# Half-batch units in a fused chunk-select attention and gated FFN kernel: one fp32 transpose of keys and queries, chunk bounds taken from PSUM

## The chip, the cores and the metric

The kernel runs on one core of a Trainium2 chip. Times are device microseconds (us). Verdicts use a 95% interval of the ratio to the kernel before, measured on the same chip in the same rounds; "faster" needs more than 2%. A ratio is the mean time of one kernel's runs over that of the other's in the same rounds, so it is not quite the ratio of the medians that are quoted beside it.

Engine names in the profile: PE is the matmul engine, PEld its weight loads, DVE the vector engine, ACT the scalar engine, POOL GpSimd, SPq the queue that issues ordinary loads. The granted clock (PEclk) is the share of its full speed that PE was allowed. PSUM is the memory in which the matmuls and transposes of this kernel leave their results; its buffers come in small pools, and a slot is one buffer of a pool. "Early" and "late" unit below mean the first and the second half of a batch's queries. Units are named 0a, 0b, 1a and so on.

## The reference

Four batches, eight heads, 768 positions of 64 numbers. Keys are grouped into 24 chunks of 32. For each query, a bound on the score of each chunk is computed from the chunk's elementwise minimum and maximum; the six chunks with the highest bound, of those that causality allows, are kept, and softmax attention runs on them alone. The result goes through a gated FFN (512 to 1536 to 512).

```python
ub = np.sum(np.maximum(q[..., None, :] * k_min, q[..., None, :] * k_max), axis=-1)
ub = np.where(causal, ub, -1e9)
top_chunks = np.argsort(ub, axis=-1)[..., -6:]
scores = np.where(sel & lower_triangle, scale * (q @ k.T), -1e9)     # cut
attn = softmax(scores) @ v
gate = 1 / (1 + np.exp(-(x @ w_gate)))                               # x: heads side by side
out = (gate * (x @ w_val)) @ w_out
```

## The kernel before

A group is one batch and four of its heads. Keys are loaded twice, once by rows and once by chunks; the second copy feeds two long DVE reductions. Queries are transposed in fp32 for the bounds and, with the keys, a second time in fp16 for the scores. The mask of rejected chunks rides inside the score matmul as 32 more rows of the contraction (rows 64 to 96 of `hk` and `hq`). The FFN of batch b is mixed into the attention of batch b+1, so, apart from a few matmuls that run ahead, it begins when both groups of batch 0 are done.

```python
def load(g):                                       # one group: q, k, v by rows, k again by chunks
    nc.sync.dma_start(d["kc"], k[b, h0:h0 + 4].rearrange("h (c s) d -> (h c) s d", s=CH))
    for n, src in (("q", q), ("k", k), ("v", v)):
        for h in range(4):
            nc.sync.dma_start(d[n][:, :, h, :], src[b, h0 + h].rearrange("(sb p) d -> p sb d", p=128))

def chunk_bounds(g):                               # two DVE instructions over [96, 64, 32]
    nc.vector.tensor_reduce(kmm[:, 0:64], kv, AX.X, ALU.max)
    nc.vector.tensor_reduce(kmm[:, 64:128], kv, AX.X, ALU.min, negate=True)

# ... q_signs: fp32 transposes of q, relu(q) and relu(-q); feats: fp16 transposes of k and q (cut)

for g in range(NG):
    if g % 2 == 0 and g > 0:
        ffn = ffn_tasks(g // 2 - 1)                # the FFN of the whole batch before
        parts = [ffn[:len(ffn) // 2], ffn[len(ffn) // 2:]]
    a = attend_tasks(g, prep_tasks(g + 1))         # scores and values, preparation of the next group
    merge(a, parts[g % 2])                         # PE order: attention and FFN, mixed
for c, t in ffn_tasks(B - 1):
    t()                                            # the last FFN has nothing to mix with
```

The softmax here doesn't subtract the row's maximum and nothing guards it: scores larger than these inputs give would overflow.

## Time and profile before

| | before |
|---|---|
| median time | 393.64 us (393.15 to 393.91, 3 runs) |
| PE busy over the span | 320.2 us, 81% |
| first FFN product complete (its first matmul ran at 68.5) | 110.5 us |
| one group in the steady part | 41.35 us, PE busy 37.3 |
| FFN with nothing beside it, at the end | about 47 us |

These are lines of the page of the kernel before: busy time by engine, then PE, the granted PE clock in tenths, and the DMA engines, each in 40 equal slices of the span (a digit 9 is 90% or more).

```profile
span 393.6 us, 6906 instructions
PE 320.2 (81%) x2696; PEld 197.2 (50%) x2696; DVE 230.0 (58%) x486; ACT 204.6 (52%) x393; POOL 73.5 (19%) x77
...
PE   1071549287598999799979998799999999999996
PEclk9996557856969999999999999999999999999999
DMA  9999999297920964433615010002000100100102
```

The first eleven slices (108 us) are the start. There PE is partly idle, the DMA engines are full for seven slices, and the clock is low in much of it. From the twelfth slice PE reads 7 to 9 up to the last.

The windows view gives the same by stretches. Its columns are the length of the stretch, then busy time (and instruction count) of PE, PEld, DVE, ACT and POOL, the granted clock, the DMA share and GB/s. The first stretch is the start, the second one group of the steady part, the third the FFN at the end.

```profile
core 0: us, PE busy (x) PEld busy (x) DVE busy (x) ACT busy (x) POOL busy (x), PEclk, DMA share, GB/s
0.00:112.00 112.00, 57.58 (x502) 38.40 (x503) 76.61 (x156) 48.12 (x86) 35.86 (x43) 0.77 1.03 187
178.90:220.25 41.35, 37.30 (x338) 22.93 (x337) 27.81 (x60) 25.23 (x50) 8.08 (x7) 1.00 0.41 97
344.00:391.00 47.00, 45.98 (x260) 25.13 (x257) 13.29 (x24) 15.34 (x30) 0.00 (x0) 1.00 0.09 34
```

In the start PE is busy half the time; a steady group has 37.3 of 41.35 us; the end 46.0 of 47.

The groups view shows the two reductions of one steady group: busy us, mean ns of one.

```profile
L140 DVE TENSOR_REDUCE kmm_2829<-kc_2777 96x64 f32<-96x2048 f32 x1 | 3.7, 3680 | 0.0
L141 DVE TENSOR_REDUCE kmm_2829<-kc_2777 96x64 f32<-96x2048 f32 x1 | 3.6, 3583 | 0.0
```

### The profile page before, as it was taken

Reading aid. Unit: us, or ns where it says so; the run is one execution under the profiler, and the core shown is the slowest. Engines: PE = TensorE matmul, PEld = TensorE weight load, DVE = VectorE, ACT = ScalarE, POOL = GpSimd, SP = SyncE. Lnnn points to the kernel's source line nnn. Section 1 sums busy time; section 2 is a strip of 40 time slices with the busy share of each in tenths; the row PEclk is TensorE's granted clock in tenths of the full one; section 3 lists DMA queues with packets and bytes.
Section 4 is the critical chain, followed back from the end, with each engine's and each line's share of the span. In section 5 each row is a group of like instructions: output and inputs, shape, how many; then the busy total and the mean of one; then the engine's idle time right before and its main releaser. Section 6 shows DMA issues by size and latency. Waiting matters only on the chain.

```text
span 393.6 us, 6906 instructions
## 1 busy us (share of the span) xinstructions
PE 320.2 (81%) x2696; PEld 197.2 (50%) x2696; DVE 230.0 (58%) x486; ACT 204.6 (52%) x393; POOL 73.5 (19%) x77
## 2 busy tenths in 40 slices
PE   1071549287598999799979998799999999999996
PEld 0040335164464656455645555465666566565552
DVE  4947629967949745855596658664556544142230
ACT  1150446266576548555556656655876466332331
POOL 4504143232312051003300230011101001000000
PEclk9996557856969999999999999999999999999999
DMA  9999999297920964433615010002000100100102
GB/s 181 217 214 214 208 212 195 66 217 148 214 62 15 226 156 108 101 62 86 155 42 120 28 55 0 2 2 80 2 2 27 55 2 1 55 27 28 54 2 80
DMA packets 84400, 36.62 MB, mean 93 GB/s; under 512 B 75920, under 2 KB 80528, under 8 KB 83600
## 3 DMA queue, kind: packets, MB, share of 16 engines
q1 hardware_dynamic: 79616, 31.47, 37.3%
q0 software_dynamic: 4752, 4.72, 7.2%
q8 instruction: 21, 0.34, 0.4%
q14 instruction: 11, 0.09, 0.1%
HBM read 34.60 MB, written 6.29 MB: 104 GB/s over the span
## 4 chain that ended last, share of the span: by engine, by line
PE 58%; DVE 17%; ACT 8%; issue 6%; SPq 5%; DMA 4%; POOL 1%; ACTq 0%; DVEq 0%; POOLq 0%
SPq L125 5%; DMA k_177<-in_k_dram 3%; DMA kc_151<-in_k_dram 2%; DVE kmm_1096 L140 1%; DVE kmm_209 L140 1%; DVE kmm_721 L141 1%; DVE kmm_1096 L141 1%; DVE kmm_209 L141 1%; PE o_0_0_2626 L296 1%; PE o_0_0_3781 L296 1%; PE o_384_0_3203 L296 1%; PE o_384_0_2048 L296 1%; PE o_0_0_1471 L296 1%; PE o_384_2_4783 L296 1%; PE o_384_1_4298 L296 1%
## 5 line engine op out<-in xcount | busy, mean ns | idle before, releaser
L287 PEld LDWEIGHTS <-wv_146 128*128 128x128 f16 x384 | 37.9, 99 | 28.3 <-issue 4.2
L281 PEld LDWEIGHTS <-wg_145 128*128 128x128 f16 x384 | 35.7, 99 | 23.2 <-issue 6.7
L153 PE MATMUL qT_0_212<-ident_103,q_148 128*128 128x128 f32 x5 | 1.3, 426 | 8.4 <-DMA q_148<-in_q_dram 8.4
L243 PEld LDWEIGHTS <-hk_123 96*128 96x128 f16 x48 | 4.8, 122 | 3.8 <-issue 2.9
L153 PE MATMUL qT_1_227<-ident_103,q_148 128*128 128x128 f32 x5 | 1.3, 427 | 5.9 <-DVE qcat_1_221 L160 5.9
L153 PE MATMUL qT_0_369<-ident_103,q_176 128*128 128x128 f32 x5 | 1.3, 426 | 5.8 <-DMA q_176<-in_q_dram 5.8
L140 DVE TENSOR_REDUCE kmm_1096<-kc_1044 96x64 f32<-96x2048 f32 x1 | 3.7, 3667 | 3.7 <-PE kct_756 L146 3.7
L272 PE MATMUL xps_1_671<-ident_108,xnat_400 128*128 128x128 f16 x6 | 0.8, 307 | 6.1 <-DVE xnat_400 L265 6.1
L140 DVE TENSOR_REDUCE kmm_209<-kc_151 96x64 f32<-96x2048 f32 x1 | 3.6, 3591 | 3.8 <-DMA kc_151<-in_k_dram 3.8
L272 PEld LDWEIGHTS <-xnat_400 128*128 128x128 f16 x24 | 2.1, 120 | 7.2 <-DVE xnat_400 L265 6.9
L243 PEld LDWEIGHTS <-hk_135 96*128 96x128 f16 x48 | 4.3, 109 | 2.4 <-issue 1.1
L290 DVE SCALAR_TENSOR_TENSOR hg_384_0_4595<-gate_384_0_4588,v_384_0_4590 128x384 f16<-128x384 f16 x1 | 0.6, 553 | 8.5 <-PE v_384_0_4590 L287 8.5
L243 PEld LDWEIGHTS <-hk_125 96*128 96x128 f16 x48 | 4.5, 110 | 1.9 <-issue 0.5
L193 PEld LDWEIGHTS <-ap_140 128*128 128x128 f16 x20 | 1.5, 106 | 7.7 <-DVE ap_140 L187 6.1
L264 DVE RECIPROCAL rz_0_423<-pv_0_401 128x6 f32<-128x6 f32 x1 | 0.2, 195 | 8.8 <-PE pv_0_401 L261 8.8
L193 PE MATMUL apT_316<-ident_108,ap_140 128*128 128x128 f16 x5 | 0.7, 309 | 5.7 <-DVE ap_140 L187 5.7
L243 PEld LDWEIGHTS <-hk_131 96*128 96x128 f16 x48 | 4.1, 107 | 2.3 <-issue 1.1
L243 PEld LDWEIGHTS <-hk_133 96*128 96x128 f16 x48 | 4.3, 108 | 1.8 <-issue 0.2
L153 PEld LDWEIGHTS qT_0_212<-ident_103,q_148 128*128 128x128 f32 x5 | 0.9, 220 | 8.3 <-issue 8.3
L140 DVE TENSOR_REDUCE kmm_359<-kc_179 96x64 f32<-96x2048 f32 x1 | 3.6, 3597 | 2.4 <-DMA kc_179<-in_k_dram 2.4
L261 PE MATMUL pv_0_401<-v_141,att_0_335 128*128 128x65 f16 x21 | 1.3, 244 | 4.5 <-POOL att_0_335 L249 4.5
L243 PEld LDWEIGHTS <-hk_127 96*128 96x128 f16 x48 | 4.2, 106 | 1.6 <-issue 0.2
(2400 smaller groups left out, 1201.9 us busy)
## 6 DMA issues: line engine op xcount, KB each, us to landing
wg_145<-in_moe_w_gate_dram POOLq DMA_DIRECT2D x3, 512.0 KB, 9.8
wv_146<-in_moe_w_val_dram POOLq DMA_DIRECT2D x3, 512.0 KB, 7.7
wo_147<-in_moe_w_out_dram POOLq DMA_DIRECT2D x3, 512.0 KB, 12.9
kc_151<-in_k_dram SPq DMA_DIRECT2D x1, 768.0 KB, 5.9
q_148<-in_q_dram SPq DMA_DIRECT2D x4, 192.0 KB, 6.6
k_149<-in_k_dram SPq DMA_DIRECT2D x4, 192.0 KB, 6.5
v_150<-in_v_dram SPq DMA_DIRECT2D x4, 192.0 KB, 7.3
kc_179<-in_k_dram SPq DMA_DIRECT2D x1, 768.0 KB, 17.0
```

Source lines behind the costliest of these rows:

```text
L125: nc.sync.dma_start(d[n][:, :, h, :], src[b, h0 + h].rearrange("(sb p) d -> p sb d", p=128))
L140: nc.vector.tensor_reduce(kmm[:, 0:64], kv, AX.X, ALU.max)
L141: nc.vector.tensor_reduce(kmm[:, 64:128], kv, AX.X, ALU.min, negate=True)
L153: nc.tensor.transpose(ps[:, 128 * i:128 * i + 128], d["q"][:, i + 1, 2 * pr:2 * pr + 2, :].rearrange("p h d -> p (h d)"), ident32)
L193: nc.tensor.transpose(ps[:, 128 * i:128 * i + 128], apt[g % 2][:, i, :, :].rearrange("p h c -> p (h c)"), ident16)
L243: nc.tensor.matmul(ps[:, o:o + w], hk[:, 128 * jb:128 * jb + 128], hq[:, i0:i0 + w], start=True, stop=True)
L261: nc.tensor.matmul(ps[:, ib, :], at[:, c:c + 128], v16s[g % 2][:, jb, h, :], start=(jb == 0), stop=(jb == ib))
L272: nc.tensor.transpose(ps[:, 128 * ib:128 * ib + 128], xnat[b][:, ib, 128 * c:128 * c + 128], ident16)
L281: nc.tensor.matmul(gp, wg16[:, c, 128 * fb:128 * fb + 128], xT[(b, c)][:, t0:t0 + TCH], start=(c == 0), stop=(c == 3))
L287: nc.tensor.matmul(vp, wv16[:, c, 128 * fb:128 * fb + 128], xT[(b, c)][:, t0:t0 + TCH], start=(c == 0), stop=(c == 3))
L290: nc.vector.scalar_tensor_tensor(hg, gate, 1.0, vp, ALU.add, ALU.mult)
L296: nc.tensor.matmul(op, hgl[(b, t0, fc)][:, 128 * tb:128 * tb + 128], wo16[:, fc, :], start=(fc == 0), stop=(fc == NFB - 1))
```

## The change

The unit becomes half a batch of queries for all eight heads. Keys and queries are transposed once, in fp32. The chunk maximum and minimum are reduced straight from the PSUM of the key transpose, so the second key load and the fp16 casts of keys and queries on POOL go. The FFN of a unit is mixed into the attention of the next unit. The score matmul keeps its mask rows.

```diff
-def load(g):   # kc by chunks, then q, k, v of four heads
+def load(u):   # k, q, v of 384 rows, all heads
+    for n, src in (("k", k), ("q", q), ("v", v)):
+        for i in range(HB):
+            nc.sync.dma_start(t[:, i], src[u.b, :, r:r + 128].rearrange("h p d -> p h d"))
-    nc.vector.tensor_reduce(kmm[:, 0:64], kv, AX.X, ALU.max)
-    nc.vector.tensor_reduce(kmm[:, 64:128], kv, AX.X, ALU.min, negate=True)
+def keys_t(u, p, pool):             # a pair of heads
+    ps = pool.tile([128, T], F32, tag="ps", ...)
+    for x in range(HB):
+        nc.tensor.transpose(ps[:, 128 * x:128 * x + 128], u.k[:, x, 2 * p:2 * p + 2, :]..., ident32)
+    for e, op in enumerate((ALU.max, ALU.min)):
+        nc.vector.tensor_reduce(out=u.kmm[:, p, e, :], in_=pv, op=op, axis=AX.X)
+    nc.scalar.copy(hk[0:64, 2 * p, u.rows], ps[0:64])
+    nc.vector.tensor_copy(hk[0:64, 2 * p + 1, u.rows], ps[64:128])
+# queries_t: the same for q; relu on ACT, min(q, 0) on DVE, two fp16 copies into headQ on ACT
# pools of PSUM, shortened:
-pff bufs=3, psc bufs=3, pbig bufs=1 (1024 fp32 wide)
+pff bufs=3, psc bufs=3, ppr bufs=2  # ppr: preparation and output transposes
+for c, t in prep_tasks(units[0], [ppr, psc]):
+    t()
+load(units[1])
 for i in range(3):
     load_w(i)                       # gate and value weights, cast to fp16 by DMAs of the POOL queue
+fill_kept(1, nc.gpsimd)
 for i in range(3):
     load_wo(i)
+for i, u in enumerate(units):
+    a = attend_tasks(u, prep_tasks(units[i + 1], [ppr]))
+    merge(a, prev)
+    prev = ffn_tasks(u)
```

## The prediction

> **What bounds it now.** Two regimes. The timeline in slices: until about 112 us PE is mostly idle (windows: 28.8 us busy of the first 60) while the DMA rings move 210 GB/s; batch 0 is attended alone, because FFN work exists only after a whole batch. The granted clock is 0.5 to 0.84 between 30 and 120 us. From 112 us PE is the limit: in the chain of waits the iterations end every 41.35 us, PE busy 37.3 of it, ACT 25.2, DVE 27.8. The missing 4 us are largely in-order waits behind DVE: two chunk reductions of 3.6 us each (96x2048), then the sign copies, appear on the chain together with "issue" gaps of 2 us. The last 47 us are the FFN of batch 3, PE 94 to 100% busy.
>
> **What changes.**
> 1. Units of half a batch: FFN work can start after the first unit (6 of 21 causal blocks per head) instead of after batch 0. The trailing FFN halves from about 47 to 24 us; that is no gain in PE work, but the filler moves to the start, where PE idles. Largest term.
> 2. The second load of keys goes (8 x 768 KB, 6.3 of 31.5 MB on the hardware queue). First unit needs 2.4 MB instead of 3.1, though the six weight loads now start at once and compete with it (4.7 MB at about 210 GB/s with the rest).
> 3. DVE loses 16 reductions of 3.6 us (57 us) and gains 64 reductions of 384 columns from PSUM. [...] (640 columns 0.83 us), so estimate 0.55 us each, 35 us. More important: no DVE instruction is over about 1 us, so FFN gates no longer queue behind 3.6 us.
> 4. PE: 192 fp16 transposes (55 ns each warm) and 80 fp32 ones (109 ns) become 192 fp32 ones: 19 to 21 us, neutral. Scores, values, FFN unchanged: about 36.7 us of work per unit, as now.
> 5. ACT gains: query copies 64 x 0.49, smaller pieces; from 205 to about 250 us (estimate). In a late-half unit ACT is near 38 us against PE 39; this caps part of the gain. POOL loses 16 casts of 1.46 us.
>
> **Sum (estimate).** First-unit prep and attention, DMA-bound: FFN work begins near 46 us, instead of 112; first late unit at about 50. Then 3 late units of 43 us, 3 early ones of 36.5 us, the last late unit 38 us, trailing FFN and store 26.5 us, less some FFN already done, plus about 4 us of cold clock: 357 us, 9% less. PE busy about 310 us.
>
> Predicted 357 us; 8 in 10 within 343 to 374. Faster by over 2%: 0.94; within 2%: 0.04; slower: 0.02.
>
> **What would show it.** Step 1: first FFN matmul at 40 to 52 us; last FFN-only stretch 24 us. Step 2: hardware queue near 25 MB; first score near 30 us. Step 3: reductions 0.5 to 0.6 us, DVE busy near 190 us, steady PE share over 90% in units 1a to 3a. Step 5: ACT 240 to 260 us; early units 35 to 38 us, late ones 41 to 45.
>
> **What would make it wrong.** Slower: ACT or the two-buffer PSUM pool (preparation and output transposes share it; four readers per key tile) stalls the in-order PE, so late units take 47 us or more; the weight loads delay queries of the first unit past 25 us; the clock stays low until 100 us. Faster: a start before 40 us, or PE 95% busy in the late units.

Step 3: a ground for its 0.55 us is the trace's 0.83 us for 640 columns (a DVE instruction from PSUM in the kernel before); by columns alone that would be 0.50 us, an estimate from that one size. The sum: 50 + 3 x 43 + 3 x 36.5 + 38 + 26.5 + 4 makes the 357 us, with nothing taken off for "some FFN already done". Two of its figures are not quite what the windows view gives: in the first 60 us PE was busy 20.9 us, not 28.8, and the DMA engines moved 208 GB/s there, but 118 to 184 GB/s from 60 to 120 us. The in-order PE that it names is seen in e12, where PE waited 15.8 us for queries of unit 0b with steps of 0a behind them.

## More of the kernel before

The experiments ran in three sets of rounds on two chips, in which the kernel before had medians from 393.2 to 394.1 us, so medians of different sets are compared to about 1 us.

A causal mask is the POOL instruction that zeroes the weights of later keys.

A scheduler decides the final order on each engine.

## The result, and the profile after

| | before | after | predicted |
|---|---|---|---|
| median time | 393.68 us (4 runs) | 383.96 us (382.3 to 385.59, 4 runs) | 357 (343 to 374) |
| ratio | | 0.9755 (0.971 to 0.980) | |
| first full score group | 43.7 us | 44.35 us | near 30 |
| first score of the first late unit (0b) | | 76.8 us | about 50 |
| late unit, in the steady part | | 45.6 us | 41 to 45 |
| early unit | | 34.8 us | 35 to 38 |
| from the first late unit to the end | | 307.1 us | 307 (357 less 50) |

The kernel is faster by 2.5%, not by 9%. The last line says where to look: everything from 76.8 us on took, in sum, as long as predicted, so the whole miss of 27 us lies before it. The first full score group is read, in both kernels, as the first score matmuls that no longer wait for a mask.

The same lines of the page after the change:

```profile
span 383.9 us, 7138 instructions
PE 327.1 (85%) x2704; PEld 201.3 (52%) x2704; DVE 210.4 (55%) x600; ACT 244.9 (64%) x545; POOL 60.3 (16%) x99
...
PE   0214667799999989999899999999999999999996
PEclk9999998559999999999999999999999999999999
DMA  8999996925341934221310441000010001001002
```

PE now reads 8 or 9 from slice 9 up to the last, but it is near idle for the first three slices, and its total busy time is not lower. ACT rose from 204.6 to 244.9 us.

The windows of the changed kernel: up to the first full score group, from there to the first late unit, that late unit, and then one early and one late unit of the steady part (the boundary between those two, at about 157.3 us, is accurate to about 1 us).

```profile
core 0: us, PE busy (x) PEld busy (x) DVE busy (x) ACT busy (x) POOL busy (x), PEclk, DMA share, GB/s
0.00:44.35 44.35, 12.12 (x47) 6.10 (x48) 16.10 (x47) 10.86 (x27) 16.93 (x28) 1.00 1.10 192
44.35:76.77 32.42, 23.69 (x157) 15.44 (x157) 19.76 (x60) 19.64 (x45) 7.01 (x10) 0.82 1.05 186
76.77:122.55 45.78, 43.15 (x387) 28.11 (x386) 26.25 (x83) 34.57 (x77) 5.60 (x9) 0.91 0.38 74
122.55:157.30 34.75, 33.41 (x272) 19.93 (x269) 24.54 (x63) 24.98 (x58) 6.49 (x9) 1.00 0.53 108
157.30:202.90 45.60, 43.04 (x412) 27.49 (x410) 26.58 (x84) 35.45 (x80) 4.70 (x9) 1.00 0.22 59
```

In the steady part PE is busy 96% of an early unit and 94% of a late one, against 90% of a group before. A pair of units takes 80.35 us where two groups took 82.7. In the first 44 us, PE is busy 12 us while the DMA engines are full.

The waits of those first 80 us (engine, instruction, releaser: us in total, times, longest):

```profile
ACT qs_0a L188 <- PE qT_0a_193 L183: 26.9, 1, 26.9
PE qT_0a_193 L183 <- DMA q_0a<-in_q_dram: 12.5, 3, 6.1
PE kT_0a_156 L162 <- DMA k_0a<-in_k_dram: 11.7, 3, 7.0
```

PE waited 12.5 us for queries of unit 0a and 11.7 us for its keys. ACT sat idle 26.9 us before its first piece of work on those queries, with key copies queued behind it.

The issue lines say how long a transfer took from issue to landing (median):

```profile
wg_152<-in_moe_w_gate_dram POOLq DMA_DIRECT2D x3, 512.0 KB, 12.8
wv_153<-in_moe_w_val_dram POOLq DMA_DIRECT2D x3, 512.0 KB, 15.4
q_0a<-in_q_dram SPq DMA_DIRECT2D x3, 256.0 KB, 19.3
q_0b<-in_q_dram SPq DMA_DIRECT2D x3, 256.0 KB, 5.0
```

A query load of 256 KB of unit 0a took 19.3 us to land; one of unit 0b took 5.0 us. What differs is that the six gate and value weight loads (the first two lines) were in flight beside the first; e1 and e10 test this. SPq itself was held too: the three query loads of 0a took 12.5 us to issue, those of 0b 3.3 us, and every later load on this queue started behind them.

The timeline of PE shows the second wait in the start (start us, duration us):

```profile
46.61 0.90 PE L162 MATMUL kT_0b_335<-ident_112,k_0b 128*128 128x128 f32 x3
...
59.06 0.88 PE L183 MATMUL qT_0b_425<-ident_112,q_0b 128*128 128x128 f32 x3
...
61.01 0.53 PE L289 MATMUL g_0a_674<-xT_0a,wg_152 128*128 128x384 f16 x1
...
76.77 0.58 PE L248 MATMUL sc_0b_0_659<-hq_136,hk_130 96*128 96x128 f16 x4
```

The queries of unit 0b were issued between 31.5 and 33.7 us and take 5 us, so they lay ready at about 39 us. Their first transpose ran at 59.1 us, and the first score of 0b at 76.8.

### The profile page after: what moved, and what is told of

The parts are those of the page before. It is cut to its first block, busy times and chain, and to the rows that moved or that the text cites. A ratio compares the mean times of both kernels' runs of the same rounds, so it can differ in the third digit from the quotient of the medians.

```text
span 383.9 us, 7138 instructions
## 1 busy us (share of the span) xinstructions
PE 327.1 (85%) x2704; PEld 201.3 (52%) x2704; DVE 210.4 (55%) x600; ACT 244.9 (64%) x545; POOL 60.3 (16%) x99
## 3 DMA queue, kind: packets, MB, share of 16 engines
q1 hardware_dynamic: 78336, 25.17, 30.7%
## 4 chain that ended last, share of the span: by engine, by line
PE 60%; ACT 19%; DVE 8%; DMA 6%; issue 3%; SPq 2%; POOL 0%; ACTq 0%; DVEq 0%
DMA q_0a<-in_q_dram 5%; ACT hq_131 L191 3%; SPq L96 2%; ACT hq_136 L191 1%; DMA k_3b<-in_k_dram 1%; ACT hq_136 L234 1%; PE o_3a_4799 L304 1%; PE o_2a_3685 L304 1%; PE o_0a_1217 L304 1%; PE o_3b_5082 L304 1%; PE o_2b_4248 L304 1%; PE o_1a_2451 L304 1%; PE o_0b_1792 L304 1%; PE o_1b_3026 L304 1%; PE o_3a_4744 L304 1%
## 5 line engine op out<-in xcount | busy, mean ns | idle before, releaser
L295 PEld LDWEIGHTS <-wv_153 128*128 128x128 f16 x384 | 37.2, 98 | 28.3 <-issue 6.6
L289 PEld LDWEIGHTS <-wg_152 128*128 128x128 f16 x384 | 35.0, 99 | 16.0 <-issue 2.4
L248 PEld LDWEIGHTS <-hk_130 96*128 96x128 f16 x240 | 20.8, 107 | 11.4 <-issue 7.2
L248 PEld LDWEIGHTS <-hk_135 96*128 96x128 f16 x240 | 18.8, 97 | 8.5 <-issue 3.0
L188 ACT ACTIVATE qs_0a<-qT_0a_193 64x256 f32<-64x256 f32 x2 | 0.8, 380 | 26.9 <-PE qT_0a_193 L183 26.9
L183 PE MATMUL qT_0a_193<-ident_112,q_0a 128*128 128x128 f32 x3 | 1.4, 474 | 12.5 <-DMA q_0a<-in_q_dram 12.5
L162 PE MATMUL kT_0a_156<-ident_112,k_0a 128*128 128x128 f32 x3 | 1.4, 467 | 11.7 <-DMA k_0a<-in_k_dram 11.7
L132 POOL COPY hk_135<-epat 32x768 f16<-32x768 f16 x8 | 6.2, 822 | 0.1
L155 POOL CAST v_133<-v_0a 128x1536 f16<-128x1536 f32 x1 | 1.5, 1463 | 24.2 <-DMA v_0a<-in_v_dram 24.2
L166 DVE TENSOR_REDUCE kmm_0a<-kT_0a_156 128x12 f32<-128x384 f32 x2 | 1.0, 553 | 6.6 <-PE kT_0a_156 L162 6.6
L229 PEld LDWEIGHTS <-ap_137 128*128 128x128 f16 x20 | 1.6, 107 | 4.5 <-DVE ap_137 L223 3.8
L229 PEld LDWEIGHTS <-ap_132 128*128 128x128 f16 x20 | 1.5, 103 | 4.1 <-DVE ap_132 L223 3.4
L200 PE MATMUL ubT_0b_520<-qs_0b,kcat_129 128*32 128x384 f32 x8 | 1.5, 848 | 1.8 <-ACT hq_136 L191 1.8
L200 PE MATMUL ubT_0a_240<-qs_0a,kcat_129 128*32 128x256 f32 x8 | 2.1, 635 | 1.0 <-DVE qs_0a L189 0.5
L132 DVE COPY hk_130<-epat 32x768 f16<-32x768 f16 x8 | 2.9, 425 | 0.0
L183 PE MATMUL qT_0a_223<-ident_112,q_0a 128*128 128x128 f32 x3 | 0.9, 430 | 2.0 <-DVE hk_130 L169 2.0
## 6 DMA issues: line engine op xcount, KB each, us to landing
q_0a<-in_q_dram SPq DMA_DIRECT2D x3, 256.0 KB, 19.3
```

Of the source, the lines that this page charges most:

```text
L132: eng.tensor_copy(headK[i][64:96, h, :], epat)
L162: nc.tensor.transpose(ps[:, 128 * x:128 * x + 128], u.k[:, x, 2 * p:2 * p + 2, :].rearrange("p h d -> p (h d)"), ident32)
L183: nc.tensor.transpose(ps[:, 128 * x:128 * x + 128], u.q[:, x, 2 * p:2 * p + 2, :].rearrange("p h d -> p (h d)"), ident32)
L200: nc.tensor.matmul(ps[32 * i:32 * i + 32, 0:n], kcat[u.b % 2][:, 4 * j + i, :], u.qs[:, 4 * j + i, s0:T], start=True, stop=True)
L229: nc.tensor.transpose(ps[:, 128 * x:128 * x + 128], apt[j][:, x, :, :].rearrange("p h c -> p (h c)"), ident16)
L248: nc.tensor.matmul(ps[:, o:o + w], headK[u.b % 2][:, h, 128 * jb:128 * jb + 128], headQ[u.half][:, h, i:i + w], start=True, stop=True)
```

## The experiments

Theory D: weight loads share the DMA engines with the first loads, and their order sets the start. Theory L: the start is a chain of small dependent steps on ACT, DVE and PE, with two PSUM slots for preparation, and weights matter little. A third question is whether the steady part is limited by ACT, by PE or was limited by the long reductions.

| run | first late unit at, us | median, us | ratio to before |
|---|---|---|---|
| the change | 76.8 | 383.96 | 0.9755 |
| e1 weights after queries of 0a | 73.6 | 381.92 | 0.9690 |
| e2 no weights (wrong result) | 63.1 | 370.48 | 0.9403 |
| e3 query copies on DVE | 75.6 | 381.87 | 0.9694 |
| e4 PSUM slots | 67.1 | 374.06 | 0.9501 |
| e6 weights after queries of 0b | 75.8 | 383.95 | 0.9761 |
| e7 e6 and slots | 74.2 | 382.15 | 0.9713 |
| e8 e7 and query copies on DVE | 74.1 | 380.39 | 0.9666 |
| e9 no weights and slots (wrong result) | 54.0 | 361.74 | 0.9188 |
| e10 e7 and value casts held | 54.3 | 361.78 | 0.9197 |
| e11 e10 and query copies on DVE | 56.8 | 362.69 | 0.9212 |
| e12 weights after queries of 0a, slots, casts held | 69.2 | 377.18 | 0.9584 |
| e5 before, reductions split | | 387.14 | 0.9840 |

The first late unit's start is read from the profiled run; its span less that start is 304 to 307 us in every run of the changed kernel. So a run's total is its start plus a constant.

### e1: weights wait for the first unit's queries

```diff
 def load_w(i):
     lo, hi = 512 * i, 512 * i + 512
+    last = units[0].q[:, HB - 1, H - 1, D - 1:D]
+    nc.gpsimd.tensor_copy(wg16[:, 0, lo:lo + 1], last)   # overwritten by the load, which must wait for it
+    nc.gpsimd.tensor_copy(wv16[:, 0, lo:lo + 1], last)
     nc.gpsimd.dma_start(wg16[:, :, lo:hi], wgs[:, :, lo:hi])
```

> The changed kernel with one thing altered: the six gate and value weight loads wait until the queries of the first unit have landed. Theory D (the first unit's loads share the DMA rings with 3.1 MB of weights): the last query load lands near 9 us instead of 28, the first score group moves from 44 to about 27 us, the first late unit starts at about 60 instead of 77, total 366 to 371 us. Theory L (the chain of small dependent instructions on ACT, DVE and PE in preparation sets the start, or the first FFN waits for weights anyway): the first late unit starts no earlier than 72 us, total 379 us or more.

Measured: 381.92 us. Unit 0a's queries took 5.0 us to land, the first full score group ran at about 26 us, as theory D had it, but the first late unit moved by 3 us only. The issue lines of this run, and then one of the waits of POOL:

```profile
q_0a<-in_q_dram SPq DMA_DIRECT2D x3, 256.0 KB, 5.0
q_0b<-in_q_dram SPq DMA_DIRECT2D x3, 256.0 KB, 23.2
v_0b<-in_v_dram SPq DMA_DIRECT2D x3, 256.0 KB, 14.6
```

```profile
POOL v L158 <- DMA v_0b<-in_v_dram: 20.6, 1, 20.6
```

The slow transfers are now those of unit 0b: 23.2 us for its queries, and POOL, in order, waited 20.6 us for its values ahead of six of the eight causal masks of 0a. The collision was moved, not removed. Theory D's cause held and its consequence did not.

### e2: no weights at all

```diff
-    nc.gpsimd.dma_start(wg16[:, :, lo:hi], wgs[:, :, lo:hi])
+    nc.gpsimd.memset(wg16[:, :, lo:hi], 0.01)            # wrong result on purpose; wv16, wo16 alike
```

> Wrong result on purpose: no weight is loaded, the weight tiles are filled with a constant. This is the bound of what any reordering of the weight loads can win. Theory D: total about the same as with the weights held back, or up to 6 us less, 360 to 370 us. If the start is limited by the dependent chain after the queries land, the stretch from the last query landing to the first late unit stays near 49 us (28 to 77 in the changed kernel) and only its beginning moves.

Measured: 370.48 us, wrong result as intended; first late unit at 63.1, by the timeline of PE:

```profile
63.13 1.83 PE L248 MATMUL sc_0b<-hq,hk 96*128 96x128 f16 x10
```

Without weights the start shortens by 13.6 us. The first full score group moved from 44.4 to 31.1 us, but the stretch from there to the first late unit stayed at 32.0 us (32.4 before). The queries of 0b landed early here too, at about 21 us, so there is a second wait. The run is not a strict bound: the constant fills ran on POOL among its other work of the start, and its first full score group came 3 us later than in e6 (27.9 us), which holds the weights back instead. The expectation that it would stay 49 us behind the queries was loose: the queries landed near 10 us, so the stretch was about 53.

### e3: query copies on DVE

```diff
-    nc.scalar.copy(headQ[u.half][0:64, 2 * p + e, :], ps[64 * e:64 * e + 64])
+    nc.vector.tensor_copy(headQ[u.half][0:64, 2 * p + e, :], ps[64 * e:64 * e + 64])
```

> The changed kernel with the 64 query copies into the score operand on DVE instead of ACT. If ACT (35.4 of 45.6 us busy in a late unit, and on the chain of waits there) holds the late units back: they fall from 45.6 to about 44 us, and the start shortens by 2 to 4 us, total about 376 us. If PE is the limit in the steady part (94 to 96% busy): late units stay within 0.7 us and the total within 3 us of the changed kernel, 381 to 386 us.

Measured: 381.87 us. ACT fell from 244.9 to 217.5 us busy and DVE rose to 244.9. Unit 0b took 44.3 us instead of 45.8, and the rest of the span after it 260.3 instead of 261.35. Taking 27 us off ACT thus gave 1 us over the last six units and the tail, 2.5 us with unit 0b: the steady part follows PE, and ACT costs it little.

### e4: three more PSUM slots for the second unit's transposes

```diff
-    prep = prep_tasks(units[i + 1], [ppr])
+    prep = prep_tasks(units[i + 1], [ppr, pff] if i == 0 else [ppr])   # FFN slots, idle then
```

> The changed kernel with the second unit's key and query transposes given also the three PSUM slots of the FFN, idle then. If the two-slot PSUM pool stretches the time from the first score group (44 us) to the first late unit (77 us), that stretch falls from 33 to under 28 us and the total to 379 us or less. If it is the order of the dependent steps or ACT, it stays at 31 to 34 us and the total within 2 us.

Measured: 374.06 us, 10 us under the changed kernel, by one argument. The first full score group stays at 44.5 us, and the stretch from there to the first late unit falls from 32.4 to 22.6 us. The timeline of PE in this run:

```profile
32.96 0.69 PE L162 MATMUL kT_0b<-ident,k_0b 128*128 128x128 f32 x2 [0.89 <-DMA k_0b<-in_k_dram]
...
39.31 0.48 PE L183 MATMUL qT_0b<-ident,q_0b 128*128 128x128 f32 x1
...
67.10 0.82 PE L248 MATMUL sc_0b<-hq,hk 96*128 96x128 f16 x8 [0.22 <-ACT hq L234]
```

The queries of 0b are first transposed at 39.3 us, about when they land, instead of at 59.1. The first late unit starts at 67.1. This is theory L's PSUM part: 9.7 us, against 13.6 for theory D's (e2).

### e5: the kernel before, its reductions cut in four

```diff
-    nc.vector.tensor_reduce(kmm[:, 0:64], kv, AX.X, ALU.max)
+    for x in range(0, 64, 16):
+        nc.vector.tensor_reduce(kmm[:, x:x + 16], kv[:, x:x + 16, :], AX.X, ALU.max)   # min alike
```

> The kernel before, with each 3.6 us chunk reduction cut into four of a quarter, same total work on DVE. If the long reductions cost the steady part by holding FFN gates and sign copies behind them, as the prediction says: its iterations fall from 41.35 to about 39.5 us, six of them, total about 382 us. If the shorter units of the changed kernel gained it otherwise: 41 us or more and the total within 3 us of before.

Measured: 387.14 us against 393.22, between the two expectations. The interval of the ratio, 0.980 to 0.988, leaves out 1. The first `out` matmul of the first FFN half moved from 136.4 to 130.6 us, and three steady groups took 122.2 us where they took 125.0: 40.7 instead of 41.7 each (in both the granted clock was under 1.00 in one of the three: 0.96 over that group in the kernel before, 8 tenths in one slice of the page of e5). So the length of the reductions cost the kernel before about 1 us per group and more in its start. That is real, but less than the prediction took it for.

### e6, e7, e8: weights wait for the second unit's queries

```diff
-    last = units[0].q[:, HB - 1, H - 1, D - 1:D]
+    last = units[1].q[:, HB - 1, H - 1, D - 1:D]         # and the same for the three loads of wo16
```

e7 adds the slots of e4; e8 adds also the copies of e3.

> The changed kernel with all nine weight loads held until the second unit's queries have landed, so that neither of the first two units' keys and queries shares the rings with weights. Holding them back for the first unit's queries alone only moved the wait: the second unit's queries then landed near 50 us. Theory D2 (bytes in wrong order): second unit's queries land near 20 us, the first late unit starts at 61 to 65 us as without any weights (63), total 370 to 374 us. If the weights then come too late for the first FFN work: total 378 us or more, with waits of PE for weights between 50 and 75 us.

> The same, and the second unit's transposes also get the three idle FFN slots of PSUM. Slots alone gave 10 us and weights alone (bound) 13.5 us. If they remove two separate waits in a row: first late unit at 50 to 55 us, total 360 to 365 us. If both remove the same wait (either lets the second unit's transposes run early): 58 us or later and total 368 us or more.

> The same, and the query copies on DVE. Alone that gave 2 us. If the chain on ACT in the start is what remains: 2 to 5 us under the run without it; if weights arriving are what remains: within 1 us.

Measured: 383.95, 382.15 and 380.39 us. All three missed, and none of the stated alternatives was the reason. In e7 the queries of 0b took 5.2 us to land and were first transposed at 25.3 us, yet the late unit began at 74.2. One of the waits of PE in e7, and its timeline of POOL:

```profile
PE pv_0a L272 <- POOL att_0a L258: 18.5, 1, 18.5
```

```profile
40.47 0.52 POOL L258 TENSOR_SCALAR_AFFINE_SELECT att_0a<-att_0a 128x384 f16<-128x384 f16 x1 [0.75 <-ACT att_0a L255]
60.51 1.47 POOL L159 CAST v<-v_1a 128x1536 f16<-128x1536 f32 x1 [19.52 <-DMA v_1a<-in_v_dram]
61.92 1.00 POOL L258 TENSOR_SCALAR_AFFINE_SELECT att_0a<-att_0a 128x384 f16<-128x384 f16 x2
```

Four of the eight masks of 0a had run by 41 us. Then the scheduler's order had POOL cast the values of unit 1a, two units ahead, and these now came behind the weights: POOL waited 19.5 us with the remaining four masks of unit 0a queued behind the cast (the expectation of e10 says six, which is the count of e1), and PE waited 18.5 us for a mask. In e6 the same cast waited 18.6 us. The gain was traded for a new wait. Of the 1.8 us between e7 and e8, 1.5 come after the first late unit's start: again what moving copies to DVE gives there.

### e9, e10, e11, e12: the two repairs together, and their order

e9 is e2 with e4. e10 is e7 with one more hold, so that the early cast cannot stand in front of the masks. e11 adds e3. e12 is e10 with the weights held for 0a's queries only, as in e1 (the output weights not held).

```diff
 def cast_v(u):
+    if u in units[2:4]:
+        c = 2 * D if u is units[2] else H * D
+        nc.gpsimd.tensor_copy(v16s[u.b % 2][:, u.qa, 0, 0:1], units[1].x[:, 0, c - 1:c])
     nc.gpsimd.tensor_copy(v16s[u.b % 2][:, u.qa:u.qb, :, 0:D], u.v)
```

> Wrong result on purpose (no weights loaded), with the three extra PSUM slots for the second unit's transposes. Bound of both repairs together. Each alone moved the first late unit from 77 to 63 (no weights) and 67 us (slots). If they are two separate waits: first late unit at 52 to 55 us, total 360 to 363 us. If they take away the same wait: 60 us or later, total 368 to 371 us.

> All weights held until the second unit's queries have landed, extra slots, and the value casts of the third and fourth unit held until values of the second are done. In the run without that last part GpSimd, in order, waited 19.5 us for values of the third unit ahead of six causal masks of the first. If that wait took the gain: first late unit at 52 to 58 us, total 361 to 367 us. If the weights now come too late: PE waits for weights at 40 to 55 us and the total stays over 372 us.

> The same, with query copies on DVE: 1 to 3 us under the run without, 359 to 365 us.

> Weights held only for the first unit's queries, extra slots, value casts held. If the order of bytes is what matters, the second unit's queries again land near 50 us, the first late unit starts near 68 us and the total is 374 to 378 us, over the run that holds weights for both units. If only the first unit's landing and the slots matter: within 2 us of that run.

Measured: e9 361.74, e10 361.78, e11 362.69, e12 377.18 us. The timeline of PE in e9:

```profile
53.97 0.82 PE L248 MATMUL sc_0b<-hq,hk 96*128 96x128 f16 x8 [0.22 <-ACT hq L234]
```

The two repairs are separate waits: no weights took 13.6 us off the start, slots 9.7, both 22.8. Holding the weights back (e10, correct result) reaches what having none reaches. The page, the windows and the issue lines of e10:

```profile
span 361.0 us, 7153 instructions
PE 322.5 (89%) x2704; PEld 199.6 (55%) x2704; DVE 213.8 (59%) x600; ACT 244.0 (68%) x545; POOL 62.5 (17%) x110
...
PE   3365878999999999999999999999999999999996
```

```profile
core 0: us, PE busy (x) PEld busy (x) DVE busy (x) ACT busy (x) POOL busy (x), PEclk, DMA share, GB/s
0.00:54.31 54.31, 31.96 (x203) 20.30 (x204) 39.58 (x108) 30.00 (x72) 24.47 (x46) 1.00 1.23 199
54.31:99.76 45.45, 42.37 (x386) 27.67 (x386) 26.05 (x83) 34.49 (x77) 5.76 (x10) 0.92 0.68 139
99.76:361.00 261.24, 248.14 (x2121) 151.64 (x2117) 148.19 (x410) 179.47 (x397) 32.29 (x54) 1.00 0.20 51
```

```profile
q_0a<-in_q_dram SPq DMA_DIRECT2D x3, 256.0 KB, 5.1
q_0b<-in_q_dram SPq DMA_DIRECT2D x3, 256.0 KB, 5.1
```

The stretch from the second unit on (45.45 us) and the rest (261.2 us) are those of the changed kernel; only the first shrank, from 76.8 to 54.3 us. The wait of PE in e12, and its first full score group:

```profile
PE qT_0b L189 <- DMA q_0b<-in_q_dram: 15.8, 3, 6.5
```

```profile
46.07 1.54 PE L254 MATMUL sc_0a<-hq,hk 96*128 96x128 f16 x9 [0.16 <-ACT hq L240]
```

With weights held for 0a only, PE waits 15.8 us for the queries of 0b, and the run ends 15 us after e10. (The last of those queries were transposed at 44.6 us; "near 50" had been expected.) So it is the order of the bytes for both units that counts. The slots are part of this wait: with them the transposes of 0b stand in PE's order ahead of the last selection steps of 0a, so that 0a's own first full score group came only at 46.1 us, against 26.0 in e1. e11 was expected to be under e10 and was not: its late unit starts 2.5 us later, and the part after it is 2.3 us shorter. Why it starts later was not tested: DVE, which took the copies over, is the busiest engine in the start (39.6 of 54.3 us in e10), and the granted clock was lower (up to the first late unit 1.00 in e10 and about 0.85 in e11, an estimate from its mean of 0.966 over the span and its 0.92 and 1.00 after that start).

e10 is the fastest version: 361.78 us, 8.0% under the kernel before and about 22 us under the changed kernel.

A rival is the granted clock, which differs from run to run in the start: from the first full score group to the first late unit it was 0.82 in the changed kernel, 5 and 6 tenths in the two slices from 46.7 to 65.4 us in e4, and 1.00 in e10. It does not explain the gains. e4 gained 9.7 us at the lower clock; and in e7 and e10, alike up to there, the same two copies on ACT ran at 44.56 and 44.55 us, with a clock of 5 tenths in the two slices from 19 to 38 us in e7 and of 1.00 in e10. It may be a part of the smaller differences: the four runs of the changed kernel took 385.6 us at a mean clock of 0.971 and 382.3 to 383.4 at 0.986 and 0.987.

## Why the prediction was wrong

- **The step that failed: "First-unit prep and attention, DMA-bound: FFN work begins near 46 us, instead of 112; first late unit at about 50."** The first late unit began at 76.8 us and FFN work in earnest only after it (a few FFN matmuls ran from 61 us on, outside the 40 to 52 us that step 1 named as its test; the first product was complete at 81.5 us, against 110.5 before). The term was mis-sized by 27 us, and the total missed by 27 us. Of these, e9 and e10 take back 22.8 and 22.5 us; the last 4 us, 54 against 50, stay open. The prediction added bytes, 210 GB/s and a preparation time. It did not ask which bytes land first, nor how many PSUM slots the second unit's preparation has while the FFN slots stand empty.
- **Its first part.** "First score near 30 us" was 44. The queries of 0a landed at 28 us, beside 3.1 MB of weights. The prediction named this among what would make it wrong ("the weight loads delay queries of the first unit past 25 us"), and gave it no weight in the sum. e2 shows 13.6 us for weights in all, with the first full score group back at 31.1 us, and e10 and e12 show that both first units must be ahead of them. A 256 KB load took 5.1 us with no weight load in flight (e10) and 19.3 us beside the weight loads; how the engines divide their time between the two queues was not shown.
- **Its second part.** From the first score group to the first late unit the prediction allowed 20 us; it took 32.4. e4 shows 9.7 us of it to be PSUM slots. The prediction named the two-slot pool as a risk for late units; it bit in the start, where no FFN work could fill the wait.
- **The steady part was right in sum.** Three late units of 45.8, 45.6 and 45.6, three early ones of 34.75, 34.8 and 34.7, the last late one of 39.6 and the tail of 26.3 us make 307.2; the prediction's terms after the start, with 4 us for a low clock, made 307. That the sums agree is in part luck: each late unit was 2.6 us longer, over its stated range of 41 to 45, each early one 1.8 us shorter, under its range of 35 to 38, and the errors cancel. ACT cost little of it: moving copies off ACT gave 1.5 to 2.5 us after the start (e3, e8, e11).
- **Step 2** held in its bytes: the hardware queue moved 25.17 MB instead of 31.47.
- **Step 3** held in size: a reduction from PSUM takes 0.555 us, as the groups view shows:

```profile
L166 DVE TENSOR_REDUCE kmm_2a<-kT_2a_1923 128x12 f32<-128x384 f32 x2 | 1.1, 555 | 0.4 <-PE kT_2a_1923 L162 0.4
```

The estimate was 0.55; the 0.83 us for 640 columns that it names stands in the trace (0.827 us). DVE was busy 210.4 us instead of the expected 190. That "the missing 4 us are largely in-order waits behind DVE" was too strong as far as the length of the reductions goes: e5 gives about 1 us per group. It left their total work on DVE in place, so what that work costs is not shown.
- **Step 4** held roughly: PE busy went from 74.6 us per two groups to 76.4 per two units, not quite neutral; in all PE was busy 327.1 us, not "about 310". **Step 5** held: ACT at 244.9 us, within 240 to 260.

Left open: what the remaining 54 us of start in e10 could be cut to. e9, without any weights, has the same 54 us, so it is not weights. Nor is it, after the first 21 us, the landing of keys and queries: POOL's wait for the last query of 0b ended at 20.8 us. The other 33.5 us are work and waits among the engines; no run takes them apart.

## What to carry to other kernels

Cutting work into smaller units gave 2.5% here, and 8.0% once the first two units' inputs arrived first and the second had more slots: list what the DMA queues hold at the start in order of first need, and hold later bytes (weights) with a real data dependency until the first two units have landed. A start has its own limits, so look for slots of a later stage that are idle then and lend them (9.7 us here, e4). When a repair moves nothing, look at the waits of every engine again before dropping the theory: here two correct repairs were hidden by a cast on POOL standing in front of causal masks.

## Rates and orders that the traces show

- A 256 KB load of 256-byte rows on the hardware queue took 5.1 us with no weight load in flight (e10) and 19.3 us (23.2 in e1) beside 512 KB casting loads of the POOL queue.
- POOL kept its order: 19.5 us behind one cast in e7. An order that cost nothing became a stall once a transfer was moved: in the changed kernel the cast of 0b's values, behind two of the eight masks of 0a, ran at 47.29 us without a wait, and in e1, behind two masks again, POOL waited 20.6 us for those values.
- A 128x128 fp16 transpose of the kernel before took 314 ns (median) in each of the six groups of them before 60 us and 218 to 219 ns in the steady part. In a row they go faster than that: in the steady part six fp16 ones advanced PE by 0.34 us (57 ns each, before) and three fp32 ones by 0.33 us (110 ns each, after), but in the start of the changed kernel three fp32 ones took 0.64 us (213 ns each), with a granted clock of 1.00 in both.
- A reduction along a strided axis in SBUF: 2048 fp32 elements per partition took 3.6 us (1.76 ns each, estimated as time over elements), where 384 contiguous ones from PSUM took 0.555 us (1.45 ns each, fixed cost included in both). The quarters of e5, 512 elements, took 1.015 us, which makes the slope about 1.70 ns per element (estimate from the two sizes).
